# Sliding-window attention and a gated two-layer network in one kernel: unread products ahead of the first transposes, a transpose one block later, value loads behind keys and queries

## The chip, the cores and the metric

The kernel runs on one core of a Trainium2 chip. The metric is the device time of one execution in microseconds (us). Before the change, three runs gave 285.0 us in the median, from 283.83 to 285.83.

## The reference

Eight batches with eight heads of 576 positions and 64 dimensions go through attention in a window of 32 positions to each side. The result, as 4608 rows of 512, goes through two weights with the function h * sigmoid(1.702 h) between them.

```python
scores = (q @ k^T) / sqrt(64)
scores = where(|i - j| <= 32, scores, -1e9)
attn   = softmax(scores)
x      = (attn @ v) as [4608, 512]
h      = x @ w_in            # [4608, 2048]
out    = (h * sigmoid(1.702 * h)) @ w_out   # [4608, 512]
```

## The kernel before

The 4608 rows are cut into 36 units of 128 rows (number u) and nine tiles of 512 rows (number t). All work stands in an order written out by hand, and every engine runs its own part of it in that order.

A unit is attended as follows. Its queries, shifted by 32 rows, meet the 128 keys of the unit and the first 64 keys of the next one. `scores` makes the products of keys and queries on TensorE and the exponentials on ScalarE (ACT). `band` multiplies with the mask on VectorE (DVE). `values` multiplies with the values; for half of each product it reads `ve[u % 9]`, the values as loaded, and for the other half `vo[u % 5]`, a copy that is shifted by half a unit. `odd_v` makes this copy on GpSimd (POOL), in two pieces: one from the values of unit u, one from those of unit u + 1. `norm` divides by the sums on DVE, and the result is transposed into `xT` for the network.

For the first four units and the next four (tile 1) a key or query block is loaded in one piece and transposed on TensorE (`T_first`, `T_four`); in `seed` the scores' PSUM bank is first filled with the mask as a bias, a product of the identity with 512 columns. Units 8 to 11 are loaded singly (`load_kq`) and transposed on TensorE in threes (`T_pe`). From unit 12 on, `turn` has the DMA engines transpose them, issued from SyncE's queue (SP).

The network is run by tiles: first layer in `l1_group` (four groups a tile), second layer in a list of pieces, `self.l2`, that is used up a few products at a time between other work. Both use fewer products by sums of weight and data blocks, which DVE makes. Tile 0 is run plainly, as is the first layer of its halves (`layer1_plain`); in `opening`, some blocks of tile 0 keep their products in SBUF (`kept`) so that ACT can apply the function later without changing its table in between.

All loads are issued by GpSimd, in one queue with the copies of `odd_v`. There are eight semaphores for these loads, so an issue waits for the load eight places before it. Loads are called in this order:

- `opening`: first keys and queries, values 0 to 4, the first weight (`w1`) in pieces, copies for units 0 to 3, keys and queries of tile 1 (`load_four`), the rest of `w1`, values 4 to 8, the second weight (`w2`) in four quarters, copies 4 to 7, then for u = 8 to 11 `fetch(u)`: queries u, keys u + 1, values u + 1.
- `first_layer1`, for n = 0 to 3: the copy 8 + n, then `fetch(12 + n)`.
- `run`: the copies 12 and 13 after `values(8)` and `values(9)`, `fetch(16)`, and later the copies 14 and 15 ahead of `back(2)`.
- `back(t)`: for each of four groups, `turn`, `fetch`, and one copy.

Queries and keys are held in five buffers each ahead of their transposes. A load into one waits for the transpose that reads what is in it.

Of the kernel before, what the change touches and what calls it, by code (L numbers as in the profile page):

```python
# [15 lines left out]
F32 = mybir.dt.float32  # L16
BF16 = mybir.dt.bfloat16
# [9 lines left out]
class _Kernel:  # L27
# [55 lines left out]
    def setup(self):  # L83
        nc, cst = self.nc, self.cst
        self.ident = cst.tile([128, 128], BF16, name="ident")
        self.identh = cst.tile([128, 128], F16, name="identh")
        self.mask = cst.tile([128, 4, SQ], BF16, name="mask")
        self.bias = cst.tile([128, 512], BF16, name="bias")
        self.w1 = cst.tile([128, 4, self.DFF], F16, name="w1")
        self.w2 = cst.tile([128, 16, self.DM], F16, name="w2")  # L90
        self.a = {i: cst.tile([128, 2, 1024], F16, name=f"a{i}") for i in (1, 2, 3, 4)}
        self.b = {i: cst.tile([128, 8, 256], F16, name=f"b{i}") for i in (1, 2, 3, 4)}
        self.k_first = cst.tile([128, 4, 64], BF16, name="k_first")
        self.v_first = cst.tile([64, self.H, 66], BF16, name="v_first")
        self.ve = [cst.tile([128, self.H, 66], BF16, name=f"ve{i}") for i in range(9)]
        self.vo = [cst.tile([128, self.H, 66], BF16, name=f"vo{i}") for i in range(5)]
        self.spark = cst.tile([128, 1], F32, name="spark")

    def setup_mask(self):

        D = self.work.tile([128, 128], F32, name="gap", tag="s7", bufs=2)
        self.nc.gpsimd.iota(D, pattern=[[-1, 128]], base=0, channel_multiplier=1,
                            allow_small_or_imprecise_dtypes=True)
        dve = self.nc.vector
        dve.tensor_single_scalar(self.ident, D, 0.0, op=ALU.is_equal)
        dve.tensor_copy(self.identh, self.ident)
        for r in (slice(0, 64), slice(64, 128)):
            d = D[r, r].rearrange("p (b s) -> p b s", b=1).to_broadcast([64, 2, SQ])
            up = int(r.start > 0)
            for blk, op in ((2 * up, ALU.is_ge), (2 - 2 * up, ALU.is_le)):  # L110
                dve.tensor_single_scalar(self.mask[r, blk:blk + 2, :], d, 0.0, op=op)
# [478 lines left out]

    SHARES = {("first", 1): (3, 0, 5, 4), ("first", 2): (3, 3, 6, 6), ("first", 3): (3, 1, 7, 7), ("last", 0): (0, 12, 6, 6),
              0: (4, 4, 6, 6), 1: (3, 3, 6, 6), 2: (0, 6, 5, 7), 3: (2, 1, 5, 4)}

    def opening(self):

        nc, dve, act, pool = self.nc, self.nc.vector, self.nc.scalar, self.nc.gpsimd
        self.setup()  # L600
        self.load_first("k", 0)
        self.load_first("q", 0)
        dve.memset(self.spark, 0.0)
        self.setup_mask()
        self.cut_mask()
        self.setup_bias()
        for t in self.ve:
            dve.memset(t[:, :, self.D:], 1.0)
        self.load_first("k", 1)
        self.load_first("q", 1)  # L610
        act.activation(self.spark, self.spark, AF.Exp)
        for u in (0, 1, 2, 3):
            self.load_v(u)
        self.load_v(4, slice(0, 1))
        self.load_w1(0, 256)
        self.load_w1(256, 256)
        self.load_w1(512)
        for u in (0, 1):
            self.odd_v(u, pool)
        self.load_w1(1024)  # L620
        for u in (2, 3):
            self.odd_v(u, pool)
        self.load_four("k")
        self.load_four("q")
        self.load_w1(1536)
        self.load_v(4, slice(1, 2))
        for u in (5, 6, 7, 8):
            self.load_v(u)
        for c in range(4):
            self.load_w2(c)  # L630
        self.T_first("k", 0, "AC", (dve, act))
        self.seed(0, "t")
        self.T_first("q", 0, ("LA", "LB"), (dve, act))
        self.seed(1, "AC")
        self.scores(0)
        self.scores(1)
        self.T_first("k", 1, ("LA", "LB"), (dve, dve))
        self.T_first("q", 1, ("B", "E"), (dve, act))
        self.seed(2, ("LA", "LB"))
        self.seed(3, "AC")  # L640
        self.scores(2)
        self.scores(3)
        self.values(0, "t")
        self.norm(0)
        self.values(1, ("B", "E"))
        self.norm(1)
        self.x_T(0, "LA", act)
        self.x_T(1, "LB", act)
        self.values(2, "t")
        self.norm(2)  # L650
        self.values(3, "AC")
        self.norm(3)
        h, n = ["LA", "LB", "A", "C", "B", "E"], [0]

        def l1(half, *fs, **kw):
            for f in fs:
                self.layer1_plain(0, f, half, h[n[0] % len(h)], **kw)
                n[0] += 1

        l1(0, 0)  # L660
        self.x_T(2, "B", act)
        self.x_T(3, "E", dve)
        l1(0, 2)
        l1(1, 0, 2)
        dve.tensor_copy(self.k_first, self.kT[0][:, :, 0:64])
        dve.tensor_copy(self.v_first, self.ve[0][0:64])
        l1(0, 4, 6)
        l1(1, 4, 6)
        for i in (3, 1, 2, 4):
            self.w1_sums((i,), 0)  # L670
        h[:], n[0] = ["LA", "LB", "C"], 0
        l1(0, 8)
        halo = self.kT[4]
        self.T_four("k", "BE", (dve, act))
        dve.tensor_copy(self.kT[4][:, :, 0:64], halo)
        l1(0, 10)
        act.activation(self.spark, self.spark, AF.Exp)  # L677
        self.T_four("q", "tA", (dve, act))
        gelus = []
        kept = [self.sb("s7", [128, 512], F32, 2) for _ in range(2)]  # L680
        room = self.sb("xs", [128, 2, 512], F32, 1, "room")
        kept += [room[:, i, :] for i in range(2)]
        l1(1, 8, later=gelus, kept=kept[0])
        l1(1, 10, later=gelus, kept=kept[1])
        for u in (4, 5, 6, 7):
            self.odd_v(u, pool)
        self.load_kq("k", 8)
        for u in (8, 9, 10, 11):
            self.fetch(u)
        h[:], n[0] = ["LB", "LA"], 0  # L690
        self.scores(4, "AC")
        self.scores(5, "t")
        l1(None, 12, later=gelus, kept=kept[2])
        self.scores(6, "BE")
        self.band(4)
        l1(None, 13, later=gelus, kept=kept[3])
        self.scores(7, "AC")
        self.values(4, "t")
        self.band(5)
        self.norm(4)  # L700
        h[:], n[0] = ["B", "E"], 0
        l1(None, 14, later=gelus)
        self.band(6)
        l1(None, 15, later=gelus)
        self.values(5, "t")
        self.norm(5)
        self.band(7)
        self.values(6, "AC")
        self.do(self.l2, 6)
        self.do(gelus)  # L710
        self.norm(6)
        self.values(7, "t")
        self.norm(7)
        self.do(self.l2, 2)
        for i in (3, 1, 2):
            self.w1_sums((i,), 1)
        self.x_T2(4, "A", act)
        self.do(self.l2, 8)
        self.x_T2(6, "t", dve)
        self.do(self.l2, 6)  # L720

    def fetch(self, u):
        self.load_kq("q", u)
        self.load_kq("k", u + 1)
        self.load_v(u + 1)

    def turn(self, u):
        self.T_dma("q", u)
# [35 lines left out]
    def back(self, t):  # L764
# [3 lines left out]
        u = 4 * t + 4  # L768
        bands = [lambda i=i: self.band(u + i) for i in range(4)] if more else []
        dv = bands[0:2]  # L770
        for n in range(4):
            self.turn(u + n + 4)
            self.fetch(u + n + 5)
            if t == 2 and n in (1, 3):
                self.values(u + n - 1, "t")
                self.norm(u + n - 1)
                self.x_T(u + n - 1)
            elif more and n in (1, 3):
                do(l2, n // 3 * 2)
                self.values(u + n - 1, "AC")  # L780
                self.norm(u + n - 1)
                if u + n < self.NU - 1:
                    self.x_T(u + n - 1)
                self.values(u + n, "t")
                self.norm(u + n)
                self.x_T(u + n)
                do(l2, 6 if n == 1 else 4)
# [21 lines left out]
    def run(self):  # L809
# [21 lines left out]
        do(more, 4)  # L831
        self.values(8, "t")
        self.values(9, "AC")
        self.odd_v(12, pool)
        self.odd_v(13, pool)
        self.fetch(16)
        self.scores(11, "BE")
        self.norm(8)
        self.band(10)
# [16 lines left out]
        self.scores(15, "t")  # L856
        do(self.x_sums(2))
        self.seed2 = dve
        self.odd_v(14, pool)
        self.odd_v(15, pool)  # L860
        late = self.back(2)
        for t in range(3, self.NT):
            self.front(t, late)
# [7 lines left out]
    def first_layer1(self):  # L871

        dv = [lambda: self.w1_sums((4,), 1)]
        for n in range(4):
            if n == 3:
                self.turn(12)
                self.turn(13)
            self.odd_v(8 + n, self.nc.gpsimd)
            self.fetch(12 + n)

            def fill(i):
                self.do(self.l2, {1: 1, 7: 1, 2: 3, 4: 3}[i])
# [55 lines left out]
```

## Time and profile before

| | |
|---|---|
| time of the profiled execution | 282.94 us |
| its span, first to last instruction | 281.2 us |
| median of three runs | 285.0 us |
| TensorE (PE) busy | 269.3 us, 96% |
| DVE, ACT, POOL busy | 212.2, 196.0, 132.1 us |
| loads issued by GpSimd | 106656 packets, 18.42 MB |
| first TensorE instruction | 6.13 us |
| last TensorE product begins | about 277.4 us |

The profile is of one execution. Its times count from the start of the span. In a timeline row the first number is the start, the second the time from the start of the row's first instruction to the end of its last; "x" is how many instructions the row merges, and the bracket tells how long the engine was idle before it and what ended that. A matmul's end is modelled, so TensorE being busy does not mean that it runs at its best rate. In the table of stages each row gives the stretch, its length, then the busy time (and count) of PE, of PE's weight loads, DVE, ACT and POOL, then the granted clock, the mean share of the DMA engines and GB/s.

### The profile page before, as it was taken

To read this page: it belongs to the slowest core of one execution; us is meant where nothing else is said; L and a number is where in the kernel's file an instruction comes from. 1 tells how busy PE (TensorE), PEld (TensorE's weight loads), DVE (VectorE), ACT (ScalarE), POOL (GpSimd) and SP (SyncE) were. 2 spreads that over 40 slices of the span, in tenths; PEclk is the share of its full clock that TensorE was granted. 3 is DMA by queue.
4 is the path that set the end of the run, shared out by engine and by line. 5 is a ranking of instruction groups with operands and counts; after the bars stand their busy time and mean duration, and the time that the engine had idled before them with its cause. 6 is when DMAs were issued, how large, how long until landed. Compare 5 with 4: busy or idle time off the path is not lost.

```text
span 281.2 us, 8890 instructions
## 1 busy us (share of the span) xinstructions
PE 269.3 (96%) x3648; PEld 222.5 (79%) x3648; DVE 212.2 (75%) x491; ACT 196.0 (70%) x344; POOL 132.1 (47%) x199
## 2 busy tenths in 40 slices
PE   1979999999999999999999999999999999999994
PEld 1568656776888888888888888888888888888883
DVE  4464698897978888888888887888788888855631
ACT  2576893989897688658875887687759775667410
POOL 8894596998798570936094619442210000000000
PEclk9999999999999999999999999999999999999999
DMA  8999999999999999999999999999943051101033
GB/s 88 167 206 197 178 207 162 191 131 155 134 187 142 204 159 183 101 201 136 190 105 211 136 153 89 194 155 167 157 52 95 2 114 21 75 2 75 2 112 115
DMA packets 150265, 37.61 MB, mean 134 GB/s; under 512 B 138064, under 2 KB 145872, under 8 KB 150224
## 3 DMA queue, kind: packets, MB, share of 16 engines
q0 software_dynamic: 106656, 18.42, 95.3%
q1 hardware_dynamic: 43120, 18.10, 37.6%
q8 instruction: 28, 0.46, 0.7%
q10 hardware_dynamic: 448, 0.52, 0.6%
q14 instruction: 13, 0.11, 0.2%
HBM read 36.83 MB, written 9.44 MB: 165 GB/s over the span
## 4 chain that ended last, share of the span: by engine, by line
PE 91%; DVE 3%; ACT 3%; issue 1%; POOL 1%; POOLq 0%; DVEq 0%
PE o L70 40%; PE h L70 39%; PE sc L70 5%; PE pv L70 4%; DVE x L328 1%; ACT p L290 1%; PE tp L177 1%; PE tp L244 1%; ACT kq L67 1%; POOL kq L152 1%; PE tp L356 0%; ACT L677 0%; PE tp L344 0%; PE tp L201 0%; DVE rec L327 0%
## 5 line engine op out<-in xcount | busy, mean ns | idle before, releaser
L459 ACT ACTIVATE g<-h 128x512 f16<-128x512 f32 x128 | 72.2, 598 | 35.3 <-PE h L70 35.0
L70 PEld LDWEIGHTS <-g 128*128 128x128 f16 x576 | 54.5, 98 | 10.1
L222 POOL COPY vo<-ve 64x264 int32<-64x264 int32 x71 | 32.1, 452 | 63.5 <-PE pv L70 54.4
L70 PEld LDWEIGHTS <-a 128*128 128x128 f16 x512 | 49.5, 97 | 10.5 <-issue 0.3
L70 PE MATMUL h<-xs,a 128*128 128x256 f16 x384 | 57.6, 272 | 0.2
L70 PE MATMUL o<-w,g 128*128 128x256 f16 (+1 forms) x320 | 55.0, 294 | 0.0
L70 PE MATMUL h<-xT,w 128*128 128x256 f16 (+1 forms) x368 | 53.6, 277 | 0.0
L70 PEld LDWEIGHTS <-w 128*128 128x128 f16 x496 | 47.6, 98 | 7.4
L70 PEld LDWEIGHTS <-gs 128*128 128x128 f16 x384 | 36.9, 98 | 4.9 <-issue 0.2
L290 ACT ACTIVATE p<-sc 128x512 bf16<-128x512 f32 x72 | 37.0, 618 | 3.3 <-PE sc L70 3.1
L70 PE MATMUL o<-b,gs 128*128 128x256 f16 x256 | 37.6, 273 | 0.0
L70 PE MATMUL o<-b,g 128*128 128x256 f16 x256 | 37.5, 273 | 0.0
L211 POOL DMA_DIRECT2D ve<-in_v_dram x40 | 34.3, 868 | 6.3 <-DMA w<-in_moe_w_out_dram 2.1
L472 DVE TENSOR_TENSOR h<-h,s 128x512 f32<-128x512 f32 x32 | 22.3, 698 | 18.4 <-PE h L70 18.2
L67 ACT COPY h<-h 128x512 f32<-128x512 f32 x32 | 18.9, 590 | 17.3 <-PE h L70 16.9
L328 DVE TENSOR_TENSOR x<-pv,rec 128x256 f16<-128x256 f32 (+1 forms) x52 | 27.4, 527 | 1.8
L141 POOL DMA_DIRECT2D qst<-in_q_dram x35 | 28.0, 801 | 0.9 <-issue 0.5
L141 POOL DMA_DIRECT2D kst<-in_k_dram x31 | 26.5, 858 | 0.6 <-DMA w<-in_moe_w_out_dram 0.6
L478 DVE TENSOR_TENSOR h<-h,s 128x512 f32<-128x512 f32 x32 | 22.4, 699 | 4.8 <-PE h L70 4.2
L298 DVE TENSOR_TENSOR p<-p,mask 128x1024 bf16<-128x1024 bf16 x32 | 22.4, 700 | 0.1
L67 ACT COPY s<-h 128x512 f32<-128x512 f32 x32 | 19.2, 599 | 1.3
L70 PE MATMUL h<-xs,w 128*128 128x256 f16 x128 | 19.2, 273 | 0.0
(87 smaller groups left out, 339.4 us busy)
## 6 DMA issues: line engine op xcount, KB each, us to landing
out_dram<-o_sb SPq DMA_DIRECT2D x33, 256.0 KB, 4.8
ve<-in_v_dram POOLq DMA_DIRECT2D x32, 128.0 KB, 6.6
kst<-in_k_dram POOLq DMA_DIRECT2D x25, 128.0 KB, 6.4
qst<-in_q_dram POOLq DMA_DIRECT2D x21, 128.0 KB, 5.9
w<-in_moe_w_out_dram POOLq DMA_DIRECT2D x4, 512.0 KB, 11.1
w<-in_moe_w_in_dram POOLq DMA_DIRECT2D x3, 512.0 KB, 9.7
qst<-in_q_dram POOLq DMA_DIRECT2D x7, 96.0 KB, 5.5
kq<-in_q_dram POOLq DMA_DIRECT2D x2, 256.0 KB, 5.8
```

Source lines behind the costliest of these rows:

```text
L67: (eng.copy if eng is self.nc.scalar else eng.tensor_copy)(out, in_)
L70: self.nc.tensor.matmul(out, lhsT, rhs, start=start, stop=stop, skip_group_check=True)
L141: self.nc.gpsimd.dma_start(t[off:off + n], src[b, :, s:s + n, :].rearrange("h s d -> s h d"))
L152: self.nc.gpsimd.dma_start(self.stage["first"][0:n // j, :, at:at + j], src[0, :, lo:lo + n, :].rearrange("h (p j) d -> p h j d", j=j))
L211: self.nc.gpsimd.dma_start(t[off:off + n, :, :self.D], self.v[b, :, s:s + n, :].rearrange("h s d -> s h d"))
L222: eng.tensor_copy(*((words(vo[64:128]), words(self.ve[u % 9][64:128])), (words(vo[0:64]), words(nxt)))[i])
L290: self.nc.scalar.activation(p[:, eo].rearrange("k h s -> k (h s)"), sc[eo], AF.Exp, scale=self.scale)
L298: (eng or self.nc.vector).tensor_mul(pv, pv, msk.to_broadcast([128, 8, 2, SQ]))
L328: dve.tensor_mul(x[:, 4 * at:4 * (at + n), :].rearrange("p (b h) d -> p b h d", b=n), acc[:, :, :, :D], r.to_broadcast([128, n, 4, D]))
L459: act.activation(g[:, f, 256 * half:256 * half + 256], bank.rearrange("p (i n) -> p i n", i=2), AF.Gelu_apprx_sigmoid)
L472: dve.tensor_add(e, b, s7)
L478: dve.tensor_add(c, b, s7)
```

## The change

Three things are done.

Four products of 128x512 on a tile of zeros, `idle`, are put in front of the first transposes. They go to bank "E", and nobody reads them. DVE sets the tile to zero between the two identity matrices.

`T_four("q")`, the transposes of tile 1's queries, moves behind the first of the two blocks of `layer1_plain` that follow it.

`fetch` can leave out the values. In `first_layer1` it does so for units 12 to 15, and comes ahead of the copy instead of behind it. `run` calls `fetch(16)` without values, then loads values 13 to 17 together, and only then makes the copies 12 and 13. The copies 14 and 15 are made behind the first `fetch` in `back(2)`.

```diff
+        self.idle = cst.tile([128, 512], BF16, name="idle")
...
         dve.tensor_single_scalar(self.ident, D, 0.0, op=ALU.is_equal)
+        dve.memset(self.idle, 0.0)
         dve.tensor_copy(self.identh, self.ident)
...
+    def keep_busy(self, n, tag):
+        junk = self.bank(tag, [128, 512], F32, "junk")
+        for _ in range(n):
+            self.mm(junk, self.idle[:, 0:128], self.idle, start=True, stop=True)
...
+        self.keep_busy(4, "E")
         self.T_first("k", 0, "AC", (dve, act))
...
-        self.T_four("q", "tA", (dve, act))
...
         l1(1, 8, later=gelus, kept=kept[0])
+        self.T_four("q", "tA", (dve, act))
         l1(1, 10, later=gelus, kept=kept[1])
...
-    def fetch(self, u):
+    def fetch(self, u, v=True):
         self.load_kq("q", u)
         self.load_kq("k", u + 1)
-        self.load_v(u + 1)
+        if v:
+            self.load_v(u + 1)
...
             self.fetch(u + n + 5)
+            if t == 2 and n == 0:
+                self.odd_v(14, self.nc.gpsimd)
+                self.odd_v(15, self.nc.gpsimd)
...
         self.values(9, "AC")
+        self.fetch(16, v=False)
+        for u in range(13, 18):
+            self.load_v(u)
         self.odd_v(12, pool)
         self.odd_v(13, pool)
-        self.fetch(16)
...
-        self.odd_v(14, pool)
-        self.odd_v(15, pool)
         late = self.back(2)
...
+            self.fetch(12 + n, v=False)
             self.odd_v(8 + n, self.nc.gpsimd)
-            self.fetch(12 + n)
```

## The prediction

> **What bounds the kernel now.** I read the page first, then TensorE's timeline of the first 34 us, GpSimd's timeline against it, and the busy time by stage.
>
> ```profile
> span 281.2 us, 8890 instructions
> PE 269.3 (96%) x3648; PEld 222.5 (79%) x3648; DVE 212.2 (75%) x491; ACT 196.0 (70%) x344; POOL 132.1 (47%) x199
> PE 91%; DVE 3%; ACT 3%; issue 1%; POOL 1%; POOLq 0%; DVEq 0%
> ```
>
> TensorE is busy for 96% of the span and makes up 91% of the chain that ended last. The stages (busy time in given stretches; first column the stretch, second its length, third PE's busy time) show where the other 12 us lie:
>
> ```profile
> 6.00:8.30 2.30, 2.17 (x34) 1.26 (x34) 1.14 (x11) 0.69 (x1) 2.30 (x3) 1.00 1.82 181
> 12.70:18.00 5.30, 3.87 (x126) 2.46 (x124) 3.12 (x9) 3.90 (x8) 4.92 (x11) 1.00 1.55 194
> 20.30:43.40 23.10, 22.91 (x360) 16.43 (x358) 16.36 (x31) 18.48 (x30) 15.80 (x23) 1.00 1.50 195
> 43.40:78.60 35.20, 35.20 (x493) 26.14 (x490) 29.75 (x63) 28.57 (x52) 29.56 (x44) 1.00 2.10 156
> 78.60:278.00 199.40, 198.82 (x2531) 171.45 (x2528) 156.07 (x361) 138.20 (x245) 68.54 (x103) 1.00 1.20 121
> ```
>
> From 20.3 to 278 us PE has 0.8 us of idle time in all. So the rest of the kernel is one block of TensorE work of fixed length, with a last store behind it. What the change can win lies ahead of 20.3 us, and it is kept only if no later PE instruction then reaches its data before it has landed. The change's first part works on the opening:
>
> ```profile
> 6.13 1.29 PE L177 MATMUL tp<-ident,kq 80*64 80x80 bf16 x32 [6.13 <-DVE ve L608]
> 7.36 1.03 PE L70 MATMUL sc<-bias,ident 128*128 128x512 bf16 x2
> 8.32 1.07 PE L177 MATMUL tp<-ident,kq 128*64 128x128 bf16 x16
> 9.32 1.03 PE L70 MATMUL sc<-bias,ident 128*128 128x512 bf16 x2
> 10.29 1.07 PE L70 MATMUL sc<-kq 64*64 64x64 bf16 x48
> 13.32 0.81 PE L70 MATMUL sc<-bias,ident 128*128 128x512 bf16 x3 [0.22 <-DVE kq L67]
> 14.06 0.70 PE L70 MATMUL sc<-kq 64*64 64x64 bf16 x48
> ```
>
> Two seeds take 1.03 us at 9.32, three take 0.81 us at 13.32; the same 48 score products take 1.07 us, then 0.70 us. TensorE runs slowly from its first instruction until some point between 11.3 and 12.7 us, although the granted-clock column says 1.00 throughout: durations show it, the column does not. Before 6.13 us PE does nothing. The releaser named there (DVE) is a semaphore long due: the weight load of the same transposes ends its wait on the DMA of the first keys.
>
> **Part 1, four products on zeros.** Added: one DVE memset (256 words a partition) between the two identity tiles, and four 128x512 products ahead of the first transposes. DVE's first identity tile is ready at 3.66 us (3.43 + 0.23). The memset has no row here; the nearest are 0.06 us for a 128x16 one and 0.55 us for the 128x128 cast behind it, and I take 0.3. So PE starts at about 4.0 instead of 6.13 us. A seed has the same shape and costs 0.43 us while PE is slow (1.03 less the 0.2 us tail, halved): 4 x 0.43 = 1.7 us, done near 5.8 us, under the wait that ends at 6.13. Cost on the path: 0; up to 0.2 if the memset takes 0.55. DVE's masks and bias slip by 0.3 us; the bias is done at 6.1 and the seeds want it at 7.36, so that is covered too.
>
> What it brings: PE activity begins 2.1 us earlier. If PE is released a given time after it begins to work, the release moves from about 12 to about 10 us. What is slow from 8.32 on and would be fast: 16 transposes (1.07, against half of the 1.11 us that 32 take at 27.25: 0.5 saved), two seeds (about 0.4), 48 scores (0.37), and part of the 32 transposes at 11.29 (1.42 against 1.11: 0.3). That is 1.6 us of PE time as upper bound; 0 is the lower one, as nothing in this trace shows what activity releases PE. Not all of it is on the path, since copies on DVE and ACT and the landing of queries stand between. With a release near 10 us the scores, the second transposes and what follows come 0.7 us earlier; with one near 8.7 us, where the transposes at 8.32 profit as well, 1.0 us. I take 0.8.
>
> The Trainium skill has a mechanism for this: "TensorE: Matmul & The Clock Gate", Part 1 (The HAM clock gate), says that the array idles at half clock and is released after a busy window of about 3.4 us that runs free of the kernel. The halved seed time above agrees; by that rule a stretch beginning at 4.0 is released, as an estimate from that page, between 7.4 and 10.8 us, and the lead would be some 1.0 us rather than 0.8 before any later limit.
>
> **What of it is kept.** GpSimd's queue shows when transfers have landed, since each of its DMA issues waits for the eighth one before it:
>
> ```profile
> 29.10 0.74 POOL L129 DMA_DIRECT2D w<-in_moe_w_out_dram  x1 [1.51 <-DMA o_sb<-in_q_dram]
> 31.49 1.48 POOL L129 DMA_DIRECT2D w<-in_moe_w_out_dram  x2 [1.65 <-DMA w<-in_moe_w_in_dram]
> 42.94 0.88 POOL L141 DMA_DIRECT2D kst<-in_k_dram  x1 [0.63 <-DMA w<-in_moe_w_out_dram]
> 45.91 0.87 POOL L211 DMA_DIRECT2D ve<-in_v_dram  x1 [2.10 <-DMA w<-in_moe_w_out_dram]
> ```
>
> These transfers follow each other through a full queue (waits of 1 to 2 us on DMAs from 22 to 46 us, none on PE), so they don't come earlier when PE does. The third quarter of the second weight has landed by about 42.7 us (the trace's landing events; GpSimd's wait for it ends at 42.94); its first product is at 43.48. So a lead over 0.8 us ends in a wait there: that is the cap. The second and the last quarter have 1.2 us and more, the first weight's last piece 1.6 (31.49 against 33.06).
>
> **Part 2, queries of tile 1 one block later.** These rows lie around it:
>
> ```profile
> 29.27 1.11 PE L201 MATMUL tp<-ident,o_sb 128*64 128x128 bf16 x32
> 30.32 1.92 PE L70 MATMUL h<-xT,w 128*128 128x256 f16 x16
> 32.43 0.70 PE L70 MATMUL sc<-kq 64*64 64x64 bf16 x48 [0.19 <-ACT kq L67]
> ```
>
> The queries landed shortly before 29.10, and their transposes begin at 29.27: any lead over 0.4 us would be lost here. One block of 8 products (1.92 / 2 = 0.96 us) ahead of them moves that margin to 1.3 us. In exchange only one block instead of two covers the copies ahead of the scores. ACT's copy begins at 31.39 behind a table load anyway, and takes 0.99 us, against transposes that would now end at 31.3: scores at 32.4 as before. DVE's copy (1.22 us) now stands behind the 0.69 us copy of the kept block: about 30.3 + 0.69 + 1.22 = 32.3. Both end within 0.1 us of today's 32.38, and both move with PE's lead, as the table load also follows ACT's earlier work. Cost: 0, at most 0.35 (1.22 less the 0.87 us of the block) where both are late.
>
> **Part 3, GpSimd's queue.** The number of instructions is unchanged: the loads of values 13 to 16 (five DMAs, as 13 is split) leave their places behind the keys of their turn, and with 17, which follows the keys 17 already, they come after the keys 17; the copies of odd values 8 to 11 move behind the keys and queries of their turn, and 14 and 15 behind the next fetch. An issue is 0.9 us, a copy pair 0.9. Nothing is queued on PE. Keys 16 gain most: their load, at 66.85, stands behind three value loads (1.4 + 0.9 + 0.9 us of issue), but in the new order waits for a key transpose on SP's queue, so I put it 2.3 us earlier. They are transposed last on SP (issued at 73.09, 5 us to landing: 78.0), and the scores that read them start at 78.64. That margin of 0.6 us would have been the next limit under a lead of 0.8; now it is 2.5 to 3. The moved loads: values 17 wait for PE to finish with values 8 (71.9 us), and behind them on GpSimd are odd 12, odd 13, then queries 17. With 5.9 us to landing, values 14 land near 77 and odd 13 is done at 77.5; the products reading it begin at 85.96. Queries 17 are issued near 77.5, as now. Cost on the path 0; bounds: 0 to 3 us (the rival below).
>
> **Sum.** 281.2 - 0.8 + 0 + 0 = 280.4 us of span; with the 1.7 us around it, 282.1 against 282.9 for the profiled execution. That one ran 2.1 us below the median of 285.0 (283.83 to 285.83), so I carry the difference over: 285.0 - 0.8 = **284.2 us**.
>
> **Rivals.**
> *A. No gain (285.0).* The transposes that follow the four products are not real products, and a pause of 0.3 us lies between; if only dense products release PE, 1.7 us of them change nothing and the release stays near 12 us. For it: the stretch 6.13 to 8.3, also transposes and two seeds, released nothing for 4 us more. The same page of the Trainium skill, Part 4 (PE-mode transpose), says that transposes don't count as busy in the same way; no row here separates the two. Against: the four products are as much work as all seeds before 10.3 us.
>
> *B. More than the sum (282.1).* The profiled execution may be one in which landings happened to be in time, and the 2.1 us above it in the median may be the waits at the margins of 0.4 us (queries) and 0.6 us (keys 16), or a later release. The change widens both, so all of it would go: 285.0 - 2.1 - 0.8. For it: margins that small, a spread of 2 us. Against: nothing here shows where the slower ones lost time.
>
> *C. Slower (288).* Values 14 and 15 come late. They are now loaded behind the keys and queries 12 to 17, and odd 13 blocks GpSimd until they land. It decides if a value load takes over 14 us from its issue at 71: the median is 5.9 and the longest here 9.2, 13.0 for a weight. Then the products at 85.96 wait some 1 to 2 us, and queries 17 to 20 behind odd 13 go out 7 to 8 us later, so that scores at 104.7 wait too: about 3 us together.
>
> **How the numbers follow.** Forecast 0.50, A 0.24, B 0.17, C 0.09. About 1% is what a measurement of this kernel can tell from no change: under 282.2 or over 287.9. Faster by over 1% comes from B and a tail of the forecast: 0.17. Slower by over 1% comes from C and a little noise: 0.09. The rest, 0.74, is within 1%. The range of 281.8 to 286.4 holds the forecast, A and B; C's far part and the outer tails are left out.
>
> **What would show it.** Right: four products from about 4.0 us that end before 6.1; the seeds' or scores' duration falling to the short value before 11 us; the first product on h near 17.3 instead of 18.22; the wait at 43.5 below 0.3 us; no PE wait at 78.6 or 86. Part 1 is wrong if the 48 scores still take 1.07 us; the cap is wrong if the lead at 47 us is over 1 us; part 3 is wrong if PE waits for a copy of odd values.

## The result, and the profile after

The changed kernel takes 285.28 us in the median of 20 runs (284.31 to 287.31); the kernel before, run beside it on the same chip, takes 283.76 us (282.74 to 286.65). The ratio is 1.0047, with an interval of 1.0028 to 1.0066: slower by 0.3 to 0.7%, where 0.8 us less had been forecast. (Before's 20 runs lie 1.2 us below the three that the forecast started from.) Here and below, a run more than 1.5% above the fastest of its kernel is in no ratio and no count of the clock (2 of the 12 of part 3 alone, one each in four other experiments, one of before's 35 in one set).

The page after: the span, the busy times, the granted clock in 40 slices of 7.1 us, the chain that ended last.

```profile
span 283.3 us, 8897 instructions
PE 271.8 (96%) x3652; PEld 223.3 (79%) x3652; DVE 211.8 (75%) x492; ACT 195.9 (69%) x344; POOL 131.4 (46%) x199
PEclk9979999999999999999999999999999999999999
PE 92%; ACT 2%; DMA 2%; issue 1%; DVE 1%; POOLq 0%
```

PE is busy 2.5 us longer with only four more products, and the third slice of the clock shows a 7. The stages after, in the columns of the table of before:

```profile
6.00:8.30 2.30, 2.17 (x34) 1.26 (x34) 1.19 (x11) 0.69 (x1) 2.30 (x4) 1.00 1.82 180
12.70:18.00 5.30, 3.40 (x114) 2.23 (x114) 2.94 (x8) 3.39 (x8) 4.91 (x11) 1.00 1.56 194
18.00:20.30 2.30, 2.00 (x31) 1.48 (x24) 1.93 (x6) 1.86 (x3) 2.30 (x4) 0.57 1.24 205
20.30:43.40 23.10, 22.91 (x357) 16.78 (x356) 14.88 (x29) 18.92 (x31) 15.55 (x23) 0.97 1.51 195
43.40:78.60 35.20, 35.20 (x487) 25.80 (x486) 29.89 (x62) 27.74 (x51) 28.48 (x41) 1.00 2.06 160
78.60:278.00 199.40, 198.06 (x2528) 170.74 (x2527) 156.15 (x362) 139.11 (x247) 69.04 (x106) 1.00 1.28 118
```

The clock is 0.57 from 18.0 to 20.3 us (1.00 before), PE was busy for 0.5 us less between 12.7 and 18 us, and for 0.8 us less behind 78.6. PE's timeline of the opening (a row is start, duration, line, operation, count, idle time before it and its releaser):

```profile
4.00 1.89 PE L70 MATMUL junk<-idle 128*128 128x512 bf16 x4 [4.00 <-DVE idle L107]
6.13 1.29 PE L179 MATMUL tp<-ident,kq 80*64 80x80 bf16 x32 [0.25 <-DMA kq<-in_k_dram]
9.32 1.03 PE L70 MATMUL sc<-bias,ident 128*128 128x512 bf16 x2
10.29 1.07 PE L70 MATMUL sc<-kq 64*64 64x64 bf16 x48
11.29 1.16 PE L179 MATMUL tp<-ident,kq 128*64 128x128 bf16 x32
16.02 0.34 PE L346 MATMUL tp<-identh,x 128*128 128x128 f16 x3 [0.78 <-DVE x L330]
17.25 0.44 PE L346 MATMUL tp<-identh,x 128*128 128x128 f16 x5 [0.90 <-issue]
```

The four products lie where they were put, under the wait for the first keys. The seeds at 9.32 and the scores at 10.29 are as slow as before. The last rows of the same stretch before were these:

```profile
16.17 0.83 PE L344 MATMUL tp<-identh,x 128*128 128x128 f16 x6 [0.78 <-DVE x L328]
17.26 0.29 PE L344 MATMUL tp<-identh,x 128*128 128x128 f16 x2 [0.26 <-DVE x L328]
18.22 1.03 PE L70 MATMUL h<-xT,w 128*128 128x256 f16 x8
```

The transposes of x now begin 0.15 us earlier, stop after three for 0.90 us under "issue" (time in which the engine waited for nothing that the profile shows), and the first product on h starts at 18.63 (18.22 before). The other stop of this execution:

```profile
78.91 0.38 PE L70 MATMUL o<-b,gs 128*128 128x256 f16 x2
80.47 0.38 PE L70 MATMUL o<-b,gs 128*128 128x256 f16 x2 [1.19 <-issue]
```

PE's lag follows from rows that both traces have. It is 0.41 us at the first product on h; 1.24 us at 77 us (four products on `o` at 77.22 before, at 78.46 after), where 0.83 comes from the slow clock behind 18.3; 2.59 us at the next scores (78.64 before, 81.23 after), behind the stop; and 2.1 us at the end. So this one execution puts the loss into the opening and one stop at 79, and none on the loads of part 3. GpSimd's timeline, though, has changed:

```profile
65.78 0.88 POOL L143 DMA_DIRECT2D kst<-in_k_dram  x1 [3.23 <-DMA kT<-kst]
69.41 4.91 POOL L213 DMA_DIRECT2D ve<-in_v_dram  x6
76.30 0.40 POOL L224 COPY vo<-ve 64x264 int32<-64x264 int32 x1 [0.60 <-DMA ve<-in_v_dram]
83.55 0.88 POOL L143 DMA_DIRECT2D qst<-in_q_dram  x1
```

Before, keys 16 and queries 18 went out without a wait:

```profile
66.85 0.89 POOL L141 DMA_DIRECT2D kst<-in_k_dram  x1
81.73 0.88 POOL L141 DMA_DIRECT2D qst<-in_q_dram  x1
```

After, GpSimd waits 3.23 us for a key transpose ahead of keys 16, then 0.60 us for values 14, and queries 18 go out at 83.55. The experiments had to say which of these the 20 runs pay for.

### The profile page after: what moved, and what is told of

It is laid out like the page before. It is cut to its first block, busy times and chain, and to the rows that moved or that the text cites. A ratio compares the mean times of both kernels' runs of the same rounds, so it can differ in the third digit from the quotient of the medians.

```text
span 283.3 us, 8897 instructions
## 1 busy us (share of the span) xinstructions
PE 271.8 (96%) x3652; PEld 223.3 (79%) x3652; DVE 211.8 (75%) x492; ACT 195.9 (69%) x344; POOL 131.4 (46%) x199
## 4 chain that ended last, share of the span: by engine, by line
PE 92%; ACT 2%; DMA 2%; issue 1%; DVE 1%; POOLq 0%
PE o L70 40%; PE h L70 39%; PE sc L70 5%; PE pv L70 4%; DMA kq<-in_k_dram 2%; PE tp L179 1%; PE tp L346 1%; PE tp L246 1%; ACT kq L67 1%; ACT xT L67 1%; PE tp L358 0%; ACT L685 0%; PE tp L203 0%; DVE x L330 0%; DVE kq L67 0%
## 5 line engine op out<-in xcount | busy, mean ns | idle before, releaser
L224 POOL COPY vo<-ve 64x264 int32<-64x264 int32 x71 | 31.3, 441 | 64.1 <-PE pv L70 54.2
L70 PE MATMUL h<-xT,w 128*128 128x256 f16 (+1 forms) x368 | 54.7, 282 | 0.3 <-ACT xT L67 0.3
L474 DVE TENSOR_TENSOR h<-h,s 128x512 f32<-128x512 f32 x32 | 22.4, 699 | 17.6 <-PE h L70 17.4
L67 ACT COPY h<-h 128x512 f32<-128x512 f32 x32 | 18.8, 589 | 17.3 <-PE h L70 16.9
```

Of the source, the lines that this page charges most:

```text
L67: (eng.copy if eng is self.nc.scalar else eng.tensor_copy)(out, in_)
L70: self.nc.tensor.matmul(out, lhsT, rhs, start=start, stop=stop, skip_group_check=True)
L224: eng.tensor_copy(*((words(vo[64:128]), words(self.ve[u % 9][64:128])), (words(vo[0:64]), words(nxt)))[i])
L474: dve.tensor_add(e, b, s7)
```

## The experiments

Each ratio is to the kernel before, run beside it, with a 95% interval; medians as "this kernel / before". "The row reached" is the first PE instruction of a new block of code, explained with the first group. The two theories: (1) the opening costs the time, because four more products shift the program against the blocks in which PE's instructions are loaded, and the pause brings the slow clock; (2) the late values cost it, through GpSimd's queue and the DMA engines.

**The opening.** The page counts PE's own code among the transfers:

```profile
q8 instruction: 28, 0.46, 0.7%
```

That is 28 transfers of 16 KB (0.46 MB) for 7304 matmuls and weight loads, about 260 each. Counted in blocks of 256, with PE's semaphore instructions counted too, the pauses below fall on a boundary: those at 17.25 and 80.47 us in the changed kernel, and shorter ones at 78.55, 77.28 and 36.29 us in three kernels further down, all stand at the same place of a block. In the DMA records, a transfer starts between 1 us before and 6 us after PE has entered the block ahead of it, and PE runs the first instruction of the new block 1.2 us or more after it has landed. One boundary lies in the transposes of x. Before, PE reaches it at 17.26 us and the block has landed at 15.63. After, it lies eight instructions earlier in the program: reached at 16.14, landed at 15.82, run at 17.25.

*The four products alone.*

```diff
+        dve.memset(self.idle, 0.0)
...
+        self.keep_busy(4, "E")
```

> The four products on zeros alone; transposes of the queries and loads stay as before. Theory 1 (instruction blocks): PE's instructions arrive in blocks of 256, whose first is row 192, then 448, 704 and so on, and eight more instructions at the front put row 448 into the first transposes of x, at about 16.1 us, before its block is there (before the change it was reached at 17.26). Expected: a pause of 0.9 to 1.2 us inside the transposes of x near 16.1 us, block load ending near 15.8 and the next product 1.4 us later; no pause near 79 us; slower by 0.8 to 1.3 us where the clock holds, more where it drops. Theory 2 (the products themselves, by an earlier or later change of the clock): no pause at row 448; time moved only by the clock. Theory 3 (parts 2 and 3 are what costs): same as before within 0.3 us.

Ratio 0.9993 (0.9968 to 1.0018), 283.85 / 283.97 us. The profile has the pause and the slow clock of the whole change:

```profile
16.06 0.34 PE L346 MATMUL tp<-identh,x 128*128 128x128 f16 x3 [0.78 <-DVE x L330]
17.26 0.44 PE L346 MATMUL tp<-identh,x 128*128 128x128 f16 x5 [0.85 <-issue]
```

Yet over the runs nothing is lost. Theory 1 is right on the place and wrong on the price.

*The same eight instructions without the work: four tiny products.*

```diff
+            self.mm(junk[0:32, :], self.ident[:, 0:32], self.ident[:, 0:8], start=True, stop=True)
...
+        self.keep_busy(4, "E")
```

> Four tiny products (32x8 on the identity, eight instructions) where the change has four products of 128x512; nothing else changed, no tile of zeros. Theory 1 (instruction blocks): the same pause near 16.1 us as with the wide products, and slower by 0.8 to 1.3 us, although PE does no work worth naming before 6.1 us. Theory 2 (clock by the wide products): as before the change, within 0.3 us, no pause. Theory 3: as before.

Ratio 0.9998 (0.9972 to 1.0024), 284.18 / 283.97 us. The pause is there without any work on 128x512 (row reached at 15.71), so it belongs to the number of instructions:

```profile
15.59 0.34 PE L344 MATMUL tp<-identh,x 128*128 128x128 f16 x3 [0.78 <-DVE x L328]
17.24 0.69 PE L344 MATMUL tp<-identh,x 128*128 128x128 f16 x5 [1.31 <-issue]
```

*One float32 product in place of the four (the diff is against the four).*

```diff
-        self.idle = cst.tile([128, 512], BF16, name="idle")
+        self.idle = cst.tile([128, 512], F32, name="idle")
...
-        self.keep_busy(4, "E")
+        self.keep_busy(1, "E")
```

> Before, with one product of 128x512 on zeros in float32 in the place of the four in bfloat16: one instruction more on PE instead of eight, and some 1.7 us of work in the same place if it takes four times as long. Theory 1: row 448 is reached behind the wait for x as before, so no pause, and the time is that of before within 0.3 us, or up to 0.8 us faster if the work releases the clock earlier. Theory 2 (the work itself costs): slower by about the same as with the four products.

Ratio 0.9991 (0.9966 to 1.0016), 283.98 / 283.97 us. In the trace the float32 product is two matmuls with two weight loads (the row at 4.24 has x2, and takes 2.08 us), so the boundary moves by four instructions and not by one, as had been expected. The row is reached at 16.11, run at 17.26, with a pause of 0.93 us that the expectation ruled out; over the runs no gain, no loss.

*64 tiny products in place of four tiny ones, which move the boundary by 128 instructions, out of the transposes.*

```diff
-        self.keep_busy(4, "E")
+        self.keep_busy(64, "E")
```

> Before, with 64 tiny products (32x8, 128 instructions) ahead of the first transposes, in PE's wait before 6.1 us; nothing else. Theory 1 (instruction blocks): row 192 is now reached near 7.4 instead of 11.0 us, the block of row 448 is loaded some 3 us earlier, and no pause is left between 16 and 17.3 us: the transposes of x end about 0.5 to 1 us earlier whatever the clock does, the next block limit (row 704, the old row 576) lies near 20.5 us; faster than before by 0.3 to 0.9 us in all, or same if that later limit takes it back. Rival (the pause there is a wait for x on VectorE, as the trace names it): the transposes of x and the second half of values keep their times, and the time is that of before.

Ratio 1.0002 (0.9977 to 1.0026), 284.47 / 284.29 us. The row is reached at 14.32 and there is no pause; but the clock rose only at 12.67 us, so there was no lead to keep.

*Five products of ones, which leave no gap ahead of the transposes.*

```diff
+        dve.memset(self.idle, 1.0)
...
+        self.keep_busy(5, "E")
```

> Part 1 alone, with five products instead of four and ones instead of zeros, so that PE has no pause between them and the first transposes. If dense, nonzero work counts for the release of the clock from its first product at 4.0 us, the release falls between 7.4 and 10.8 us; in the runs so far, with four products on zeros or without any, it fell between 9.6 and 12.9 us, 3.5 to 6.8 us behind the first transposes at 6.1. A release before 9.5 us would show that this work counts; one after 10.8 us that it doesn't; between, nothing. In time: as before within 0.4 us in either case, since the block of row 448 holds PE until about 17.2 us.

Ratio 0.9988 (0.9961 to 1.0016), 283.29 / 283.68 us. Here the clock rises early, at 8.16 us; the seeds at 7.72 show it, 0.80 against 1.03 us:

```profile
7.72 0.80 PE L70 MATMUL sc<-bias,ident 128*128 128x512 bf16 x2
14.99 0.28 PE L346 MATMUL tp<-identh,x 128*128 128x128 f16 x2 [0.43 <-DVE x L330]
16.73 0.49 PE L346 MATMUL tp<-identh,x 128*128 128x128 f16 x6 [1.46 <-issue]
```

The lead of 1.2 us at the transposes of x ends as a pause of 1.46 us at the boundary. An early clock is not enough.

*62 tiny products and two of ones: boundary moved by 128 instructions and early work together.*

```diff
+        self.shift_rows(62, "B")
+        self.keep_busy(2, "E")
```

> Before, with 62 tiny products (32x8) and then two of 128x512 on ones ahead of the first transposes, 128 instructions in all. If the block of row 448 is what takes the lead that an early release of the clock gives: row 192 is reached near 7.2 us, that block is there by 13.5, and in a run with a release before 10 us the transposes of x end by 16.6 instead of 17.3 us; 0.3 to 0.9 us faster than before over many runs. If something else takes it (the loads that land at 42.7 us and after, or transposes on SP): the transposes end early, and the time is the same within 0.4 us.

Ratio 1.0006 (0.9979 to 1.0033), 283.71 / 283.92 us. No pause (row reached at 14.18), but the clock rose at 11.12 us and the last transposes of x waited for x until 17.18. At a later boundary, at 77.28 us, PE stops for 0.48 us.

**Parts 2 and 3.** *Both, without the four products.* The diffs of parts 2 and 3 are those of the change.

> Parts 2 and 3 without the products: PE's rows keep their numbers. Theory 1: no pause near 16 us. The pause of 1.4 us near 79 us (row 2240) is either part of the moved loads (the block's load then again ends near 79 us, over 3 us behind the crossing of row 1984 at about 73.3) and costs 1.0 to 1.5 us, or it came from the shift by eight rows and is gone: then the time is that of before within 0.3 us. Theory 3 (parts 2 and 3 are what costs) wants slower by 1.3 us or more with the pause at 79 us.

Ratio 1.0053 (1.0025 to 1.0082), 285.34 / 283.97 us: the whole loss. PE does not stop at 79 us; the waits on its timeline are these, where before has none:

```profile
105.52 0.44 PE L70 MATMUL sc<-qT,kT 64*64 64x64 bf16 x22 [1.14 <-DMA kT<-kst]
108.82 0.61 PE L70 MATMUL h<-xs,a 128*128 128x256 f16 x4 [0.57 <-DVE xs L389]
```

*Part 2 alone.*

```diff
-        self.T_four("q", "tA", (dve, act))
...
         l1(1, 8, later=gelus, kept=kept[0])
+        self.T_four("q", "tA", (dve, act))
```

> Only the transposes of tile 1's queries one block later. Theory L (the moved loads cost it, part 3): the same as before, within 0.3 us, and no wait of PE at 104 us. Rival Q (the transposes cost it): slower by 1 us or more, with a wait of over 0.5 us ahead of the scores near 32 us.

Ratio 0.9989 (0.9965 to 1.0012), 284.31 / 284.29 us: nothing.

*Part 3 alone.*

> Only the moved loads and copies on GpSimd. Theory L: slower than before by 1.0 to 1.8 us, like parts 2 and 3 together; GpSimd waits 2 to 3 us near 63 to 66 us for the transpose of keys 13 ahead of the load of keys 16, waits again for values near 77, and keys 20 are transposed 2 us or more later than before, so that PE waits near 104 us for them, or near 79 us for its block of instructions. Rival Q: same as before.

Ratio 1.0044 (1.0014 to 1.0075), 285.83 / 284.29 us. GpSimd, DVE and PE, three timelines of this kernel:

```profile
65.72 0.87 POOL L142 DMA_DIRECT2D kst<-in_k_dram  x1 [3.67 <-DMA kT<-kst]
76.26 0.40 POOL L223 COPY vo<-ve 64x264 int32<-64x264 int32 x1 [0.71 <-DMA ve<-in_v_dram]
```

```profile
108.54 0.43 DVE L389 TENSOR_TENSOR xs<-xT 128x512 f16<-128x512 f16 x1 [1.94 <-DMA xT<-x]
```

```profile
109.02 0.61 PE L70 MATMUL h<-xs,a 128*128 128x256 f16 x4 [1.09 <-DVE xs L389]
```

and in the chain of waits (start, duration, what), the step that carries it:

```profile
99.23 9.21 DMA xT<-x
```

DVE's sums for tile 3 wait for the DMA transposes of x, and PE's first layer waits for the sums. No product waits for a moved value.

*Part 3 with the values left in the line of their turn (only the copies behind the loads).*

```diff
-        self.fetch(16, v=False)
-        for u in range(13, 18):
-            self.load_v(u)
+        self.fetch(16)
...
-            self.fetch(12 + n, v=False)
+            self.fetch(12 + n)
```

> Part 3 with the values left in their places behind keys; what stays is that each turn's loads come ahead of its copy of odd values, that the loads of turn 16 come ahead of the copies 12 and 13, and that the copies 14 and 15 follow the loads of turn 17. If the late values are the cause (the copy 13 waits for values 14 with the loads of turn 17 queued behind it): the time of before within 0.4 us, no wait of GpSimd for values near 77 us. If the order of copies and loads is the cause: slower by 1 us or more as with all of part 3.

Ratio 0.9971 (0.995 to 0.9993), 283.57 / 284.29 us. The loss is gone and a little is won: the copies' new place alone costs nothing, and the loss needs the values' new place. No run moves the values and leaves the copies, so whether the values' place is enough is open.

*Part 3 as it is, with the loads of turn 20 behind the copy of its turn.*

```diff
-            self.fetch(u + n + 5)
+            hold = t == 2 and n == 3
+            if not hold:
+                self.fetch(u + n + 5)
...
+            if hold:
+                self.fetch(u + n + 5)
```

> Part 3 alone, with one more move: the loads of turn 20 (queries 20, keys 21, values 21) go behind the copy of odd values 19, which waits for PE until about 95 us, instead of ahead of it at about 91. Theory D (backlog: part 3 leaves more bytes for the DMA engines to move between 90 and 108 us, and the transposes of x on SP's queue, and of keys 20, land too late for tile 3): with these three loads out of that stretch the transposes of x issued near 97 and 99 us land by 107 us, PE has no wait of over 0.5 us between 103 and 110 us, and the cost of part 3 is gone: within 0.4 us of before, or faster. Rival B (part 3 costs by copies and values at 77 to 86 us, whatever comes later): slower by 1 us or more, as part 3 was.

Ratio 0.9995 (0.9971 to 1.002), 283.65 / 283.68 us, with late values and all. GpSimd waits as in part 3 alone, but PE and DVE do not:

```profile
65.57 0.87 POOL L142 DMA_DIRECT2D kst<-in_k_dram  x1 [2.82 <-DMA kT<-kst]
76.32 0.40 POOL L223 COPY vo<-ve 64x264 int32<-64x264 int32 x1 [0.82 <-DMA ve<-in_v_dram]
```

```profile
105.78 0.42 DVE L389 TENSOR_TENSOR xs<-xT 128x512 f16<-128x512 f16 x1
```

The two transposes of x are issued by SP a little later here than in part 3 alone, and land much earlier. SP's queue, first of part 3 alone, then of this kernel:

```profile
97.64 3.02 SPq L341 DMA_TRANSPOSE xT<-x  x2
```

```profile
98.14 3.41 SPq L341 DMA_TRANSPOSE xT<-x  x2
```

By the DMA records they land at 106.78 and 108.45 us there, at 102.60 and 104.71 here. What differs ahead of them are GpSimd's loads: queries 20 and keys 21 go out at 91.13 and 92.00 us there, at 99.89 and 100.76 here.

*The same loads held back without part 3.*

> Before, with only the loads of turn 20 behind copy 19. If part of the spread of before comes from transposes of x that land near 107 us: the upper half of the runs falls, the median is 0.2 to 0.8 us lower. If that margin holds in most runs of before: same.

Ratio 0.998 (0.9958 to 1.0001), 283.35 / 283.92 us. So holding them gains at most 0.4% by itself, and its effect on part 3 (1.0044 to 0.9995) is larger, though the two intervals do not exclude that they are alike.

*The whole change with these loads held back.*

> The whole change, and the loads of turn 20 behind copy 19. If the backlog at 90 to 108 us is what the whole change costs: within 0.4 us of before, no wait of PE between 103 and 110 us. If the pause near 79 us (the block of row 2240, loaded late) is a lasting cost of its own: slower by about 1 us, with that pause of over 1 us in the profile.

Ratio 1.0007 (0.9982 to 1.0032), 284.43 / 283.92 us: the loss is gone over the runs. The profiled execution still has one such wait (waits of PE, 60 to 115 us: sum, times, longest):

```profile
PE h L70 <- DVE xs L390: 1.7, 1, 1.7
```

So a single execution doesn't settle this wait. Part 2 alone and the 64 tiny products, which lose nothing over their runs, each show it once too (1.1 and 0.8 us).

*Part 3 with values 15 and 16 between queries 15 and keys 16, where GpSimd stood idle.*

```diff
-        for u in range(13, 18):
+        for u in (13, 14, 17):
...
-            self.fetch(12 + n, v=False)
+            self.load_kq("q", 12 + n)
+            if n == 3:
+                self.load_v(15)
+                self.load_v(16)
+            self.load_kq("k", 13 + n)
```

> Part 3 alone, but values 15 and 16 are loaded between queries 15 and keys 16, where GpSimd in part 3 waits 3 to 4 us for a buffer with nothing issued; values 13, 14 and 17 stay behind keys 17, and copy 13 still waits for values 14. If the hole in the DMA stream at 65 to 70 us is the cause (some 0.3 MB fewer landed by 70 us than before): the bytes landed by 70 us are within 0.1 MB of before, no wait at 104 to 109 us, and the time within 0.5 us of before. If the copy 13 that waits for late values 14, with the next loads behind it, is the cause: slower by 1 us or more, with that wait near 76 us kept.

Ratio 1.0023 (0.9995 to 1.0051), 284.85 / 283.68 us: between, and inconclusive. The idle time ahead of keys 16 is nearly gone, and 10.52 MB of loads have landed by 70 us (before 10.59, parts 2 and 3 10.27), but now the copies wait longer, 2.41 us for values 13 in the second piece of copy 12, and PE's waits are there again:

```profile
65.95 0.88 POOL L142 DMA_DIRECT2D kst<-in_k_dram  x1 [0.51 <-DMA kT<-kst]
75.72 1.71 POOL L223 COPY vo<-ve 64x264 int32<-64x264 int32 x3 [2.41 <-DMA ve<-in_v_dram]
```

```profile
PE sc L70 <- DMA kT<-kst: 1.4, 1, 1.4
PE h L70 <- DVE xs L389: 0.7, 1, 0.7
```

The idle stretch is therefore not shown to be the cause: with it filled, the loss is not shown to be gone.

**Versions that might beat both.** *Part 2, part 3 with values in line, loads of turn 20 held back;* and *the same with the 62 tiny products and two of ones.*

> A version meant to beat both: no products on zeros, the queries of tile 1 one block later, the loads of each turn ahead of its copy with values in line, and the loads of turn 20 behind copy 19. By theory D the transposes of x then land 1 us or more ahead of need: faster than before by 0.6 to 1.6 us, no wait of PE between 103 and 110 us. By rival B as without the last move: faster by 0.3 to 1 us.

> All that helped or did no harm: the 62 tiny and two wide products, the queries of tile 1 one block later, loads of a turn ahead of its copy with values in line, the loads of turn 20 behind copy 19. If both limits (block of row 448, backlog at 100 us) are gone: faster than before by 0.6 to 1.5 us. If the early lead is lost at the weight that lands at 42.7 us: as the version without products, 0.2 to 0.5 us faster.

Ratios 0.9988 (0.9967 to 1.0009), 283.62 / 283.68 us, and 0.9978 (0.9959 to 0.9997), 283.66 / 283.92 us. The second, like part 3 with values in line (0.9971), beats the kernel before by 0.2 to 0.3%, at the edge of what can be told, and the changed kernel clearly. The gains of the parts do not add up. In the profile of the second PE has a lead of 0.5 us on before at 34 us, and a pause of 0.62 us at a boundary, at 36.29 us, takes it.

## Why the prediction was wrong

**Part 3, "Cost on the path 0; bounds: 0 to 3 us".** This is the step that failed: measured alone, part 3 costs 1.3 us (0.44% of 284), and that is the whole loss. Two of its numbers were right: values 14 had landed by 76.3 us (near 77 was said), and no product waits for a copy. What the step left out is what comes behind. It followed each moved load to its own reader, up to 86 us, and stopped there. But the loads and the DMA transposes share engines that are well used until about 112 us (mean share before, in the column of the stage table: 1.72 from 110 to 112 us, 0.65 from 112 to 114), and a delay in GpSimd's queue can stay in that stream. Keys 16's load was noted as waiting for a key transpose; the price, 2.8 to 3.7 us in which GpSimd issues nothing, was not entered, nor the wait for values 14. The load went out 0.9 to 1.1 us earlier (66.85 before, 65.78 after), not 2.3. Queries 18 go out 1.2 to 2.7 us late (81.73 before; 82.97 in part 3 alone, 84.47 in parts 2 and 3). The transposes of x land late behind them. Before, they landed at 104.28 and 105.66 us, and PE needed the sums of them at 107.05:

```profile
96.48 3.04 SPq L340 DMA_TRANSPOSE xT<-x  x2
```

```profile
105.75 0.42 DVE L388 TENSOR_TENSOR xs<-xT 128x512 f16<-128x512 f16 x1
```

```profile
107.05 0.60 PE L70 MATMUL h<-xs,a 128*128 128x256 f16 x4
```

In part 3 alone they landed at 106.78 and 108.45; there PE was itself 0.95 us late at the scores (104.94, 104.00 before), so their later issue is not shown to come from GpSimd (part 2 alone issued them at 97.67 too). Parts 2 and 3 together are the clean case: PE was on time at these scores (103.91), the transposes landed at 106.81 and 108.25, and PE lost 2.1 us between 104 and 113 us.

**Rival C came nearest to the mechanism, by another road.** It had copy 13 blocking GpSimd and "scores at 104.7 wait too"; in parts 2 and 3 these scores wait 1.14 us. But it asked for a value load of over 14 us as the point from which it decides, and so got a chance of 0.09. The values' loads did not (first issue at 69.4, values 14 landed by 76.3); the stretch ahead of keys 16 and 0.6 to 1.6 us of waiting at copy 13 stand in their place; which of the two does it is not settled. The size was 1.3 instead of 3 us.

**Part 1, "I take 0.8".** The 48 scores at 10.29 still take 1.07 us, the prediction's own sign that this part was wrong. The clock rose at 11.48 us in the changed kernel, at 11.55 with the four products alone, at 10.51 with the whole change and the loads of turn 20 held back, and between 9.48 and 12.91 in the profiled executions without 128x512 products there: no lead that the products made can be seen. On this, rival A was right. By the Trainium skill, "TensorE: Matmul & The Clock Gate", Part 1 (The HAM clock gate), the release would have come, as an estimate from that page, between 7.4 and 10.8 us. With four products of zeros it came later in two of the three executions, with five of ones and no gap it came at 8.16, in one execution. The zeros, the gap of 0.25 us and chance are not separated by these.

**The cap.** The weight quarter at 42.7 us was to end any lead over 0.8. It never came to that: the limit lies ahead of it, at the code boundary. In every kernel with the boundary inside the transposes of x, PE goes on at 16.7 to 17.4 us, however early it came. The prediction had not looked at PE's own instructions as something that must land. The wait at 43.5 us stayed away with PE 1.26 us late there, so the cap itself was not tested: the largest lead that any profile brought to 40 us was 0.34 us.

**Part 2, cost 0.** Right: 0.9989, and no wait at the scores over 0.2 us.

**The profiled execution.** Its losses, 0.41 us at the pause, 0.83 by the slow clock and 1.35 at 79 us, are real in that execution, but the four products alone, whose profile has the first two as well, cost nothing over 12 runs. And with PE 2.58 us late at 105 us (scores at 104.00 before, 106.58 after) the late transposes (105.99 and 107.49 us here) were hidden. The losses of the two theories do not add up: whoever is late by the one doesn't wait for the other.

**Luck.** 285.28 us is near rival A's 285.0 and inside the range, though part 3 costs what A had at nothing. That is luck: the forecast started from 285.0, and before's 20 runs have a median of 283.76.

**What stays open.** Which part of GpSimd's delay makes the landings late (the idle stretch, the wait at the copies, or the new mix of loads) was not settled. The stop of 1.19 us at 80.47 was seen in one execution: its block's transfer began at 78.10 us, at 74.07 before. Part 3 with values 15 and 16 in GpSimd's idle time, which has no added products, has a shorter stop of 0.40 us at the same boundary, at 78.55. That transfer began at 74.9 to 76.9 us in the seven other profiles with part 3, and at 74.1 to 75.0 in the seven without it that have the boundary in the same place, so the delay seems to go with part 3; how is not shown.

## What to carry to other kernels

A load moved "with slack" must be followed past its own reader: here the stalls of the issuing queue were handed on to what was issued later, and the bill came some 30 us behind the last moved load. Before pricing a lead, look for the next thing that arrives by its own clock, PE's instruction blocks among them; added instructions move these boundaries for the whole program. Where one profiled execution and the runs disagree on where time went, undo the parts one by one and let the ratios decide.

## What the runs showed of the hardware

**Code arrives in blocks.** One block is 256 PE instructions; where PE arrives before it, the trace says "issue": pauses of 0.4 to 1.5 us in these profiles (1.19 at 80.47 after, 1.46 at 16.73 with five of ones, 0.40 at 78.55 in part 3 with values 15 and 16 in the idle time). Eight more instructions moved a boundary from a wait into a pause.

**The clock falls back in windows of 3.41 us.** Two stages of the changed kernel, cut where the clock changes (the columns of the stages above):

```profile
18.31:21.72 3.41, 3.11 (x21) 2.51 (x20) 2.06 (x7) 2.63 (x4) 3.41 (x5) 0.50 1.25 205
21.72:25.00 3.28, 3.28 (x32) 2.91 (x31) 2.23 (x6) 1.79 (x3) 1.17 (x2) 1.00 1.45 193
```

One such window, beginning at 16.9 to 18.4 us in 11 of the 18 profiles, takes the mean clock of a run from 1.0 to 0.994 (3.41 x 0.5 / 283 is 0.6%), so every run tells whether it had one. Of the runs of before, 43 of 139 did, with a mean of 284.59 us against 283.91 for the others. Of the four kernels that pause at the boundary (the four products alone, four tiny, one float32, five of ones) 28 of 48 did; of the three with the boundary moved by 128 instructions 3 of 35; of the changed kernel 18 of 20. But the whole change with the loads of turn 20 held back pauses there too (1.26 us) and had it in 5 of 12, and the first of the versions that might beat both, without added products or such a pause, in 7 of 12; that the pause brings the window is not shown. This was counted afterwards; no kernel was made to test it. The window may put a few tenths of a us on the changed kernel (0.59 more of the runs by 0.7 us is 0.4), but part 3 alone loses its time without it: 4 of 10 runs had the window, and the other six have a mean of 285.51 us, against 284.08 for such runs of the kernel before beside it. The Trainium skill, "TensorE: Matmul & The Clock Gate", Part 1 (The HAM clock gate), has a window of about 3.4 us that runs free of the kernel; the length agrees with the 3.41 us here, and the rise lay anywhere from 8.16 to 12.91 us.
